# Attention and token/channel mixer on one core: a hand-planned instruction order with other durations, and the odd batches' tail mask in pieces

## The chip, the cores and the metric

One core of a Trainium2 chip runs the whole program, in one launch. The metric is the device time of that launch in microseconds (us), as the median of several runs. Five engines of the core matter: TensorE (PE in the profile, its weight loads PEld), VectorE (DVE), ScalarE (ACT), GpSimd (POOL) and SyncE (SP). In this kernel GpSimd and SyncE issue DMAs and do little else. Each engine works through its own queue in order; between engines there are semaphores.

## The reference

Eight batches, eight heads, 576 positions, 64 channels a head. Attention looks back over a window of 128 positions with a bias that falls linearly with distance (its slope differs by head); a mixer over tokens and then over channels follows.

```python
scores = scale * np.matmul(q, k.transpose(0, 1, 3, 2))
bias = slopes[:, None, None] * (-np.abs(rel).astype(np.float32))[None, :, :]
mask = (rel >= 0) & (rel < window)
scores = np.where(mask, scores + bias[None], -1000000000.0)
attn = softmax(scores); x = attn @ v            # heads side by side: 512 channels
h = np.maximum(xt @ w_tok1, 0.0) @ w_tok2       # xt: x with tokens last
u = x + h.transpose(0, 2, 1)
out = u + np.maximum(u @ w_ch1, 0.0) @ w_ch2
```

(The line with softmax stands for several of the reference.) w_tok1 is 576 x 256, w_tok2 256 x 576, w_ch1 512 x 1536, w_ch2 1536 x 512.

## The kernel before

**Tiling.** A batch has 576 = 4 x 128 + 64 positions. Two batches make a pair: four blocks of 128 rows for each, and a ninth, TAIL, that holds both remainders of 64 rows, the even batch's in rows 0 to 63 and the odd batch's in rows 64 to 127. For every block of a pair the queries and keys are loaded (GpSimd's queue, L551, cast to bf16 on the way), turned (for the first pair by TensorE against an identity, L704, and copied out of PSUM, L710; for later pairs by a transposing DMA on SyncE's queue, L693), multiplied into scores for the block and the one ahead of it (L741), put through the exponential on ScalarE (L756), multiplied on VectorE by a tile of decays that is both bias and mask (L766), multiplied by the values (L799) and divided by the row sum (reciprocal L812, product L815; ScalarE can do the product too, L821). Then the token mixer: matmuls L844 and L854, a clamp at zero L862/L863, matmuls L887 and L883, sum with x L905, and a transposition (L922 and L928, or a DMA). The odd batch's 64 tail rows lie in another half than some of the weights, so the tile xt gets a copy of them in the other half (L839). The channel mixer is the main work: matmuls L1341 with clamps L1347/L1348 in the first half, tail pieces L1384, matmuls L1519 and L1429 in the second, with sums on VectorE (L1366, L1490, and the weight sums L642 and L660) that save a product of each 2 x 2 group.

**Batch 0** has a way of its own (the function opening, from L936): its q and k for two of four head pairs come in f32 over SyncE's and ScalarE's queues into the raw tiles, and VectorE or ScalarE casts them (L584); the same for its 64 tail rows (L590).

**Masks.** ScalarE makes the decay tiles `masks[:, e, i]` (L525) for the two halves e of the heads. For the odd batches, whose tail rows sit in the upper half, VectorE builds `maskt` from them: two half-width copies (L670), one full copy (L671), one memset (L672), for each e. The first pair's odd batch and all later pairs' tails read it.

**What sets the order.** No engine's order is written by hand. `plan.op(engine, cost, emit, rank, ...)` notes each instruction group with its expected duration in ns, the buffers it makes, uses and reads, and a rank; `Plan.run` then replays the machine on the host with these costs, a model of DMA queues, PSUM banks and rings of buffers, and sends out on each engine the group that can start first, ranks breaking ties (ranks under FIRST are waited for a little). The kernel is emitted in the order that this replay gives. In that replay

- a load costs its packets times PACKET = 0.813 ns on one of two modelled queues, whose clock begins at START; its result counts as there 2790 ns after;
- `after=` forbids a start before that time, RAW_AT gives such times for the raw tiles' casts;
- `other=(engine, cost, emit)` lets a second engine do it when it would end sooner;
- VectorE is free again 80 ns before an instruction's cost is over, so neighbours overlap;
- where TensorE would stand still over 250 ns before 60 us, matmuls on a zero tile are put in (`spin`, L1577).

Batch b's main work goes side by side with batch b + 1's attention and token mixer (`side`), whose ranks are spread over part of the main work's.

Of the kernel before, what the change touches and what calls it, by code (L numbers as in the profile page):

```python
# [71 lines left out]
class Plan:  # L72
# [9 lines left out]
    def op(self, eng, cost, emit, rank, makes=(), adds=(), rewrites=(), part=None, uses=(), reads=(), needs=(),  # L82
           after=0.0, order=None, bus=0.0, other=None, mode=0, behind=()):
# [6 lines left out]
        o.order, o.bus, o.other, o.mode = order, bus, other, mode  # L90
# [42 lines left out]
    def run(self):  # L133
# [28 lines left out]
        mode, turned = 0, -1e9  # L162
# [54 lines left out]
        while todo:  # L217
            best = None
            for e, c in cand.items():
                pick, early = None, None  # L220
                for o in c:
                    if e == "POOL" and o is not pool[sent]:
                        continue
                    t = max(ready[o], free[e])
                    if o.other:
                        mine, its = (o.cost, o.other[1]) if e == o.eng else (o.other[1], o.cost)
                        that = o.other[0] if e == o.eng else o.eng
                        if max(ready[o], free[that]) + its < t + mine - (0 if e == o.eng else 1):
                            continue
# [105 lines left out]
RAW_AT = [4.4e3, 5.0e3, 6.0e3, 6.6e3, 9.0e3, 8.5e3]  # L335
# [17 lines left out]
RELU = 350  # L353
# [10 lines left out]
START = 5000.0  # L364
# [5 lines left out]
DECAYS = -3e5  # L370
MORE = 1
# [18 lines left out]
def kernel(  # L390
# [197 lines left out]
    for i in range(2):  # L588
        def cast(eng, i=i, buf=last["qk"]):
            eng(out=buf()[0:R, i, :, :], in_=ends_[i * R : (i + 1) * R, :].rearrange("p (h d) -> p h d", h=H))  # L590

        plan.op("DVE", 455, lambda cast=cast: cast(dve_.tensor_copy), -1e6 + TAIL_AT, makes=last["qk"], after=RAW_AT[4 + i],
                other=("ACT", 600, lambda cast=cast: cast(act_.copy)))
# [9 lines left out]
    for item in LOADS.split():  # L603
# [7 lines left out]
        elif what == "W":  # L611
            if n == 1:
                lw1 += weights([(W1[:, 0:NC, :], w1, 512, 1640)] +
                               [(W1p[0:R, 0, :], moe_w_tok1[NC * P : S, :], 64, 250)])
            else:
                lw2 += weights([(W2[:, :, :], w2[:, :, 0 : NC * P], 256, 2300)])
        elif what == "P":
            lw1p += weights([(W1p[R:P, 1, :], moe_w_tok1[NC * P : S, :], 64, 250)])
# [48 lines left out]
    for e in range(2):  # L667
        def go(e=e):
            for i in range(2):
                dve_.tensor_copy(out=maskt[:, e, :, 0, i * R : (i + 1) * R], in_=masks[:, e, :, 0, 0:R])  # L670
            dve_.tensor_copy(out=maskt[:, e, :, 1, :], in_=masks[:, e, :, 1, :])  # L671
            dve_.memset(maskt[0:R, e, :, 1, R:P], 0.0)  # L672
        mt.append(plan.op("DVE", 1300, go, 0, after=30e3, needs=mk_ops[e]))

# [99 lines left out]
    def values(pr, blk, half, pb, rank):  # L774
# [12 lines left out]
        for es in ([[0, 1]] if both else [[0], [1]]):  # L787
# [36 lines left out]
            plan.op("DVE", 180 + 4 * (n - 1), recip, rk, makes=rt, uses=[ot])  # L824
            plan.op("DVE", 154 + 270 * n, norm, rk, part=(xb, (blk, half)), uses=[ot, rt],
                    other=("ACT", 115 + 830 * n, norms))

    def token_mix(b, rank):
# [9 lines left out]
        if xt:  # L838
            plan.op("DVE", 395, lambda: dve_.tensor_copy(out=xt()[far, :], in_=xb()[own, TAIL, :]), rank(0),  # L839
                    makes=xt, reads=[(xb, (TAIL, tk))])  # L840
# [95 lines left out]
    def opening(rank):  # L936
# [131 lines left out]
        def ends():  # L1068
# [26 lines left out]
            def value():  # L1095
                for e in range(2):
# [8 lines left out]
                    makes=rt, uses=[ots])  # L1105
# [3 lines left out]
                part=(xb, ("t", 0)))  # L1109
# [501 lines left out]
```

## Time and profile before

| what | us |
|---|---|
| median of three runs | 279.07 (278.93 to 279.22) |
| profiled execution | 279.5 |
| its span | 277.6 |
| TensorE busy | 266.5 (96%) |
| VectorE busy | 209.7 (76%) |
| ScalarE busy | 138.4 (50%) |
| GpSimd busy | 114.7 (41%) |

The time is one of the whole launch; the span goes from the first to the last instruction that the profile shows. A row of the timeline has start, length, engine, line, operation, tiles, shapes, count, and in brackets how long the engine stood idle ahead of it and what ended that. TensorE's matmuls overlap, so the length of a row goes past the start of the next. A row of a window has the window, its length, the busy time of each engine with its count of instructions, the granted TensorE clock, the mean busy share of the DMA engines and GB/s.

### The profile page before, as it was taken

The page shows a single profiled execution, that of the slowest core. Times are in us where ns is not written, and L with a number is a line of the kernel's source. Part 1 is how long each engine was busy: PE and PEld are TensorE (multiplying, and loading weights), DVE is VectorE, ACT ScalarE, POOL GpSimd, SP SyncE. Part 2 cuts the span into 40 slices and gives each one's busy share as a digit, 9 for nine tenths or more (in the row PEclk, how much of TensorE's full clock was granted, in tenths as well). Part 3 has the DMA queues.
Part 4 walks back from the last instruction along what each step waited for, and adds up shares of the span by engine and source line. Part 5 has one row for each costly group of instructions (what it writes and reads, how often), then busy time and mean ns, then how long its engine had stood idle before and what let it go on. Part 6 is the DMA issues. An engine that isn't in the chain of part 4 may idle for free.

```text
span 277.6 us, 7099 instructions
## 1 busy us (share of the span) xinstructions
PE 266.5 (96%) x2848; PEld 182.0 (66%) x2881; DVE 209.7 (76%) x489; ACT 138.4 (50%) x219; POOL 114.7 (41%) x146
## 2 busy tenths in 40 slices
PE   5989999999999999999999999999999999999994
PEld 4676566575686655585667655586667756489983
DVE  8686789996898469674978469674979469697972
ACT  6874795136971287207951087207951087205500
POOL 8988695830297008700684008800570310022000
PEclk9999999999999999999999999999999999999998
DMA  8999999999999999999899979999899820043014
GB/s 201 178 175 179 165 153 178 148 151 198 131 134 130 171 203 85 143 153 178 147 137 157 243 133 77 149 152 188 137 132 118 211 78 2 22 110 117 2 50 140
DMA packets 160337, 38.58 MB, mean 139 GB/s; under 512 B 146544, under 2 KB 159472, under 8 KB 160304
## 3 DMA queue, kind: packets, MB, share of 16 engines
q0 software_dynamic: 109968, 19.64, 90.0%
q1 hardware_dynamic: 49264, 17.83, 35.6%
q10 hardware_dynamic: 1072, 0.66, 0.8%
q8 instruction: 22, 0.36, 0.5%
q14 instruction: 11, 0.09, 0.1%
HBM read 35.85 MB, written 9.44 MB: 163 GB/s over the span
## 4 chain that ended last, share of the span: by engine, by line
PE 86%; DVE 8%; ACT 4%; issue 1%; ACTq 0%
PE ps L1519 25%; PE ps L1341 24%; PE ps L741 5%; PE ps L799 5%; PE ps L1384 4%; PE ps L844 4%; PE ps L887 4%; PE ps L1429 4%; PE ps L1265 3%; DVE WT L642 1%; ACT r L1347 1%; ACT pe L756 1%; DVE ub L905 1%; PE ps L982 1%; DVE pe L766 1%
## 5 line engine op out<-in xcount | busy, mean ns | idle before, releaser
L1347 ACT ACTIVATE r<-ps 128x512 bf16<-128x512 f32 x73 | 43.3, 602 | 76.3 <-PE ps L1341 70.4
L1341 PE MATMUL ps<-uT,WC 128*128 128x512 bf16 x304 | 77.2, 380 | 1.0
L551 POOL DMA_DIRECT2D v<-in_v_dram x36 | 30.4, 845 | 88.0 <-PE ps L799 85.6
L756 ACT ACTIVATE pe<-ps 128x1024 bf16<-128x1024 f32 (+1 forms) x64 | 55.2, 915 | 3.7 <-PE ps L741 3.0
L1341 PEld LDWEIGHTS <-WC 128*128 128x128 bf16 x324 | 28.7, 98 | 29.2 <-issue 0.9
L1519 PEld LDWEIGHTS <-r 128*128 128x128 bf16 x384 | 37.0, 98 | 9.2 <-issue 2.4
L766 DVE TENSOR_TENSOR pe<-pe,mask 128x1024 bf16<-128x1024 bf16 (+1 forms) x56 | 34.1, 618 | 9.9 <-ACT pe L756 9.4
L551 POOL DMA_DIRECT2D qk<-in_q_dram x35 | 30.2, 866 | 5.2 <-DMA qkT<-qk 3.1
L551 POOL DMA_DIRECT2D qk<-in_k_dram x35 | 30.3, 870 | 2.9 <-DMA qk<-in_k_dram 1.4
L1519 PEld LDWEIGHTS <-s 128*128 128x128 bf16 x288 | 28.1, 98 | 4.5 <-issue 0.2
L1490 DVE TENSOR_TENSOR raw<-ps,ub 128x512 f32<-128x512 f32 x27 | 18.3, 684 | 10.4 <-PE ps L1519 10.3
L815 DVE TENSOR_TENSOR xb<-ps,rt 128x256 bf16<-128x256 f32 (+1 forms) x62 | 25.2, 418 | 0.9 <-DVE rt L812 0.2
L1519 PE MATMUL ps<-WC,r 128*128 128x256 bf16 x192 | 25.4, 273 | 0.0
L1519 PE MATMUL ps<-WT,s 128*128 128x256 bf16 x192 | 24.1, 273 | 0.0
L1519 PE MATMUL ps<-WT,r 128*128 128x256 bf16 x192 | 23.7, 273 | 0.0
L799 PEld LDWEIGHTS <-pe 128*128 128x128 bf16 (+1 forms) x480 | 18.4, 99 | 7.5 <-DVE pe L766 2.1
L799 PE MATMUL ps<-v,pe 128*128 128x65 bf16 (+1 forms) x480 | 22.2, 195 | 0.0
L905 DVE TENSOR_TENSOR ub<-ps,xb 128x512 bf16<-128x512 f32 x32 | 19.7, 681 | 2.0 <-PE ps L887 2.0
L741 PEld LDWEIGHTS <-qkT 64*128 64x128 bf16 x480 | 12.8, 94 | 9.5 <-issue 6.6
L1502 POOL DMA_DIRECT2D out_dram<-raw x6 | 4.3, 717 | 34.1 <-DVE raw L1490 34.1
L1490 DVE TENSOR_TENSOR raw<-ps,raw 128x512 f32<-128x512 f32 x19 | 12.9, 688 | 7.1 <-PE ps L1519 7.0
L741 PE MATMUL ps<-qkT 64*128 64x128 bf16 (+1 forms) x256 | 16.8, 218 | 0.8
(137 smaller groups left out, 380.8 us busy)
## 6 DMA issues: line engine op xcount, KB each, us to landing
out_dram<-raw SPq DMA_DIRECT2D x21, 256.0 KB, 2.8
qk<-in_q_dram POOLq DMA_DIRECT2D x30, 128.0 KB, 5.7
qk<-in_k_dram POOLq DMA_DIRECT2D x30, 128.0 KB, 6.0
v<-in_v_dram POOLq DMA_DIRECT2D x28, 128.0 KB, 5.9
WC<-in_moe_w_ch_dram POOLq DMA_DIRECT2D x8, 384.0 KB, 7.3
out_dram<-raw POOLq DMA_DIRECT2D x6, 256.0 KB, 2.8
v<-in_v_dram POOLq DMA_DIRECT2D x16, 64.0 KB, 4.2
out_dram<-ob SPq DMA_DIRECT2D x3, 256.0 KB, 2.7
```

The lines of the kernel that those rows point to most:

```text
L551: nc.gpsimd.dma_start(out=to()[p0 : p0 + n, :, :], in_=rows(src, b, s0, n))
L741: pe_.matmul(wide(e)[:, i, kind, a:z], lhsT=ts[kb]()[e * D : (e + 1) * D, NHP + i, :], rhs=ts[blk]()[e * D : (e + 1) * D, i, a:z], start=T ...
L756: act_.activation(out=pb()[:, e, :, lo:, c0:c1_], in_=wide(e)[:, :, lo:, c0:c1_], func=ACT.Exp, scale=scale)
L766: dve_.tensor_tensor(out=o, in0=o, in1=heads(mk, es), op=ALU.mult)
L799: pe_.matmul(view()[a:z, at, i, :], lhsT=pb()[:, e, i, kind, a:z], rhs=vb()[:, h, 0 : D + 1], start=m == 0, stop=m == len(mms) - 1, skip_g ...
L815: dve_.tensor_tensor(out=x4(), in0=view()[r0:r1_, :, :, 0:D], in1=rt()[r0:r1_, 0:n, :, :].broadcast_to([r1_ - r0, n, 4, D]), op=ALU.mult)
L844: pe_.matmul(t1[j]()[:, :], lhsT=W1[:, c, j * P : (j + 1) * P], rhs=xb()[:, blk, :], start=c == 0, stop=False)
L905: plan.op("DVE", 690, lambda blk=blk, ht=ht, hs=hs: dve_.tensor_tensor(out=ub()[:, blk, :], in0=ht()[:, hs], in1=xb()[:, blk, :], op=ALU.a ...
L1341: pe_.matmul(ct()[:, :], lhsT=WC1[:, cb, t * P : (t + 1) * P], rhs=uT()[:, cb, :], start=cb == 0, stop=cb == NCB - 1)
L1347: plan.op("ACT", 600, lambda t=t, ct=ct: act_.activation(out=r2()[:, t, :], in_=ct()[:, :], func=ACT.Relu), rk, part=(r2, t), uses=[ct], o ...
L1490: dve_.tensor_tensor(out=v, in0=bk().rearrange("p (c n) -> p c n", c=2), in1=src, op=ALU.add)
L1519: pe_.matmul(bk()[:, c * HN : (c + 1) * HN], lhsT=l(t, c), rhs=w(t), start=first, stop=g == 1 and t == HK - 1, skip_group_check=True)
```

## The change

The list of loads, the tiles and the arithmetic stay. The diff (context left out) changes four things.

1. A planner item can be marked `narrow`. VectorE's next item then starts at the earliest 31 ns after the end of the one before, if either is narrow; otherwise the overlap stays. Marked are the casts of batch 0's tail rows, the divisions of tails that cover one half (the opening's and those of the first pair), and the copy to xt.

```diff
+        mode, last = 0, (False, 0.0)
...
+                    if e == "DVE" and (o.narrow or last[0]):
+                        t = max(t, last[1] + 31.0)
...
                 o.t0, free[e], o.done = t, t + max(o.cost - 80, 50), t + o.cost
+                last = (o.narrow, o.done)
```

2. Costs and times of the replay. W1 and W1p are the first token weight, W2 the second, A0 to A3 the quarters of the first channel weight. RELU is the cost of the clamp of a sum in SBUF (L1291).

```diff
-RAW_AT = [4.4e3, 5.0e3, 6.0e3, 6.6e3, 9.0e3, 8.5e3]
+RAW_AT = [4.2e3, 4.5e3, 5.7e3, 6.1e3, 7.5e3, 7.8e3]
-RELU = 350
+RELU = 295
-START = 5000.0
+START = 4300.0
...
-                lw1 += weights([(W1[:, 0:NC, :], w1, 512, 1640)] +
-                               [(W1p[0:R, 0, :], moe_w_tok1[NC * P : S, :], 64, 250)])
+                lw1 += weights([(W1[:, 0:NC, :], w1, 512, 1560)] +
+                               [(W1p[0:R, 0, :], moe_w_tok1[NC * P : S, :], 64, 270)])
...
-                lw2 += weights([(W2[:, :, :], w2[:, :, 0 : NC * P], 256, 2300)])
+                lw2 += weights([(W2[:, :, :], w2[:, :, 0 : NC * P], 256, 1560)])
...
-            lc1 += weights([(WC1[:, :, hs], c1[:, :, hs], 512, 2500 + 1400 * (n == 0))]) * (NHT // 4)
+            lc1 += weights([(WC1[:, :, hs], c1[:, :, hs], 512, 2460)]) * (NHT // 4)
```

3. The copy to xt costs 290 in place of 395 and may go to ScalarE at 600.

```diff
-            plan.op("DVE", 395, lambda: dve_.tensor_copy(out=xt()[far, :], in_=xb()[own, TAIL, :]), rank(0),
-                    makes=xt, reads=[(xb, (TAIL, tk))])
+            plan.op("DVE", 290, lambda: dve_.tensor_copy(out=xt()[far, :], in_=xb()[own, TAIL, :]), rank(0),
+                    makes=xt, reads=[(xb, (TAIL, tk))], narrow=True,
+                    other=("ACT", 600, lambda: act_.copy(out=xt()[far, :], in_=xb()[own, TAIL, :])))
```

4. The odd batches' tail mask: one item of 1300 for each e, not before 30 us, becomes four items with a rank of their own and no such time.

```diff
+MASKT = -2e5
...
-        mt.append(plan.op("DVE", 1300, go, 0, after=30e3, needs=mk_ops[e]))
-
+        got = []
+        for i in range(2):
+            got.append(plan.op("DVE", 200, lambda e=e, i=i: dve_.tensor_copy(
+                out=maskt[:, e, :, 0, i * R : (i + 1) * R], in_=masks[:, e, :, 0, 0:R]), MASKT, needs=mk_ops[e]))
+        full = plan.op("DVE", 290, lambda e=e: dve_.tensor_copy(out=maskt[:, e, :, 1, :], in_=masks[:, e, :, 1, :]), MASKT,
+                       needs=mk_ops[e])
+        got.append(plan.op("DVE", 290, lambda e=e: dve_.memset(maskt[0:R, e, :, 1, R:P], 0.0), MASKT, needs=[full]))
+        mt += got
```

More of the change, by code (lines that the diff above doesn't have):

```diff
@@ L82, in op @@
     def op(self, eng, cost, emit, rank, makes=(), adds=(), rewrites=(), part=None, uses=(), reads=(), needs=(),
-           after=0.0, order=None, bus=0.0, other=None, mode=0, behind=()):
+           after=0.0, order=None, bus=0.0, other=None, mode=0, behind=(), narrow=False):
         def many(x):
@@ L89, in op @@
         o.t0 = o.done = None
-        o.order, o.bus, o.other, o.mode = order, bus, other, mode
+        o.order, o.bus, o.other, o.mode, o.narrow = order, bus, other, mode, narrow
         o.n = len(self.ops)
```

18 lines of the change are left out of this document (6 added, 12 removed).

## The prediction, made before the changed kernel had run

> **What bounds the kernel now.** I read the page first, then busy time by stage, then the waits of TensorE, then the timelines of the stretches where it loses time.
>
> ```profile
> span 277.6 us, 7099 instructions
> PE 266.5 (96%) x2848; PEld 182.0 (66%) x2881; DVE 209.7 (76%) x489; ACT 138.4 (50%) x219; POOL 114.7 (41%) x146
> PE 86%; DVE 8%; ACT 4%; issue 1%; ACTq 0%
> ```
>
> The reader sees a TensorE kernel: 96% busy, and 86% of the chain that ended last. The profiled execution took 279.5 us, so 1.9 us lie around its span of 277.6; the median of the runs is 279.07, 0.43 below it. Sums below are made against 279.5 and span 277.6, and 0.43 is taken off at the end. The next view has busy time by stage: start and end, length, then PE, PEld, DVE, ACT, POOL, granted clock, DMA share.
>
> ```profile
> 0.00:13.00 13.00, 9.49 (x156) 7.49 (x157) 9.71 (x39) 9.46 (x18) 12.06 (x21) 1.00 1.28 193
> 13.00:27.00 14.00, 13.20 (x214) 9.82 (x211) 10.32 (x26) 8.94 (x17) 12.09 (x15) 1.00 1.79 174
> ...
> 27.00:40.00 13.00, 12.66 (x126) 7.09 (x128) 10.18 (x29) 11.22 (x18) 10.14 (x15) 1.00 1.82 157
> 40.00:46.00 6.00, 5.87 (x103) 4.14 (x101) 5.67 (x17) 5.39 (x10) 4.12 (x5) 1.00 1.33 191
> 46.00:57.00 11.00, 10.51 (x91) 7.00 (x91) 10.68 (x22) 1.85 (x4) 7.10 (x9) 1.00 2.43 148
> ...
> 60.00:91.00 31.00, 30.64 (x354) 20.84 (x358) 26.24 (x64) 18.63 (x31) 14.32 (x17) 1.00 1.71 149
> ...
> 249.00:277.60 28.60, 24.63 (x250) 22.09 (x247) 19.14 (x37) 8.96 (x16) 2.15 (x3) 0.97 0.24 78
> ```
>
> From 60 to 91 us TensorE is idle 0.36 us of 31, and the waits view has no wait of TensorE at all between 60 and 250 us. The last stage's 4 idle us are the drain behind the last matmul. So the amount of matmul sets the time after 60 us, and a new order there is worth little: I bound it at 0.3 us either way. What an order can give lies before: 0.8 us idle from 13 to 27, 0.34 + 0.13 + 0.49 from 27 to 57, and what is busy without use, which the timeline shows (start, length, engine, line):
>
> ```profile
> 30.43 0.61 PE L704 MATMUL ps<-ident,qk 128*128 128x128 bf16 x8
> 34.99 0.61 PE L704 MATMUL ps<-ident,qk 128*128 128x128 bf16 x8
> 37.62 0.61 PE L704 MATMUL ps<-ident,qk 128*128 128x128 bf16 x8
> 41.38 1.20 PE L1577 MATMUL ps<-zero 128*128 128x512 bf16 x10
> 42.70 0.66 PE L1577 MATMUL ps<-zero 128*128 128x512 bf16 x6
> 50.19 0.37 PE L854 MATMUL ps<-xt,W1p 64*128 64x512 bf16 x1 [0.38 <-DVE xt L839]
> ```
>
> L1577 is filler on a zero tile, emitted where the planner expects TensorE to have nothing. The next useful matmuls start at 42.44 and 43.43, so the two fillers stand for 1.06 + 0.73 = 1.8 us. The last row is the one wait on another engine after 30 us, 0.38. With the 0.96 idle (0.38 of it this wait) some **2.8 us** can be won from 27 to 57 at most. In 46 to 57 VectorE is busy 10.68 of 11 us and ScalarE 1.85: one engine is full beside an empty one, and the chain of waits runs over VectorE there.
>
> **The change part by part.**
>
> *Load times.* The diff starts the modelled queue of loads at 4300 instead of 5000, and makes the second token weight 740 units and the first channel weight 1440 units cheaper, at 0.813 ns a unit. All together, with small parts of 65 and 33 ns, what follows them is expected 0.70 + 0.07 + 0.60 + 1.17 + 0.1 = 2.6 us sooner. Against that stand the loads as they landed (the issue's row, then size and us from issue to landing):
>
> ```profile
> 20.34 0.91 POOL L551 DMA_DIRECT2D qk<-in_k_dram  x1
> 23.99 0.89 POOL L551 DMA_DIRECT2D qk<-in_k_dram  x1 [0.23 <-issue]
> 27.10 0.89 POOL L551 DMA_DIRECT2D qk<-in_k_dram  x1
> ```
>
> ```profile
> qk<-in_k_dram POOLq DMA_DIRECT2D x1, 128.0 KB, 7.3
> qk<-in_k_dram POOLq DMA_DIRECT2D x1, 128.0 KB, 8.7
> qk<-in_k_dram POOLq DMA_DIRECT2D x1, 128.0 KB, 8.2
> ```
>
> The keys of blocks 5, 6 and 7 landed at 27.64, 32.69 and 35.30; their transposes (L704 above) stand at 30.43, 34.99 and 37.62, so 2.8, 2.3 and 2.3 us after. An order that believes in loads 2.6 us sooner takes them 0.2 us after landing, and 0.3 us before it twice. Each of those two costs at most 0.3 us of TensorE. What it gives: scores and exponentials of batch 1 begin up to 2.5 us sooner, ahead of the stretch from 40 us in which TensorE was fed fillers. The ends are -2.3 (1.8 of filler and 0.47 idle from 27 to 46) and +0.6 (two waits, nothing won). I take **-1.0**, about half the filler, since ScalarE, which must do those exponentials, was 11.22 of 13 us busy from 27 to 40 us.
>
> *Tail mask.* Two planner items of 1300 become eight small ones, free of the rule that held them until 30 us.
>
> ```profile
> L670 DVE COPY maskt<-mask x4: 154/212/221, 29.5 to 30.3; 128x256 bf16<-128x256 bf16 x4
> L671 DVE COPY maskt<-mask x2: 280/284/288, 29.7 to 30.4; 128x512 bf16<-128x512 bf16 x2
> L672 DVE MEMSET maskt<- x2: 165/165/165, 30.1 to 30.8; 64x128 uint32 x2
> 32.67 0.56 DVE L1366 TENSOR_TENSOR s<-r 128x768 bf16<-128x768 bf16 x1 [1.75 <-ACT r L1347]
> ```
>
> The instructions are the same eight, 4 x 212 + 2 x 284 + 2 x 165 = 1.75 us, less by overlap (29.45 to 30.92). Leaving that place frees nothing by itself: the next VectorE work at 32.67 waited 1.75 us for ScalarE. It does clear the place where block 5's copy and masks now want to go. In the opening the pieces fill holes: VectorE had one of 1.79 us before 8.41.
>
> ```profile
> 8.41 0.69 DVE L960 COPY qkT<-ps 128x512 bf16<-128x512 bf16 x1 [1.79 <-PE ps L957]
> 9.13 0.87 DVE L590 CAST qk<-raw 64x512 bf16<-64x512 f32 x2
> ```
>
> The same hole takes the two casts of L590. Their sources, issued at 1.75 and 1.80 us, landed in 5.6 and 5.9:
>
> ```profile
> raw<-in_q_dram SPq DMA_DIRECT2D x1, 128.0 KB, 5.6
> raw<-in_k_dram ACTq DMA_DIRECT2D x1, 128.0 KB, 5.9
> ```
>
> That is 7.35 and 7.70, while the casts ran at 9.13. Moving them up and the pieces in leaves VectorE's load in the opening about as it was, so I cost both at **0**, hidden by that hole and by later ones of 0.2 to 0.4 us. Without that cover the pieces cost 1.5 us between 13 and 27 us, where TensorE waits on VectorE already; a gain of 0.3 is the other end, when the casts' old place goes to the copies.
>
> *What else the pieces could meet.* One copy of L839 shows it:
>
> ```profile
> L839 DVE COPY xt<-xb x7: 286/289/587, 49.5 to 207.3; 64x512 bf16<-64x512 bf16 x7
> ```
>
> ```profile
> 31.25 0.71 POOL L572 DMA_DIRECT2D W2t<-in_moe_w_tok_dram  x1 [1.68 <-DMA WC<-in_moe_w_ch_dram]
> ...
> 49.14 0.88 POOL L551 DMA_DIRECT2D qk<-in_q_dram  x1
> ```
>
> The median of seven is 289 ns; the longest, 587, is the first, at 49.55, and GpSimd was issuing a load from 49.14 to 50.02. GpSimd was busy 12.06 of the first 13 us, and idle 1.68 us up to 31.25, beside the pieces' old place. So a copy moved forward may cost 0.3 us more, and six of them 1.8. [...]
>
> *VectorE beside half tiles.* The planner let VectorE instructions overlap by 80 ns; it now keeps 31 ns between one marked narrow and its neighbours.
>
> ```profile
> 48.50 0.43 DVE L815 TENSOR_TENSOR xb<-ps,rt 64x256 bf16<-64x256 f32 x1
> 48.96 0.56 DVE L642 TENSOR_TENSOR WT<-WC,WT 128x768 bf16<-128x768 bf16 x1
> 49.55 0.59 DVE L839 COPY xt<-xb 64x512 bf16<-64x512 bf16 x1
> ```
>
> That is the truth of batch 1's tail: 48.50 + 0.43 = 48.93, the next at 48.96, and from 49.52 the next at 49.55. The hardware's time is not changed by believing it, but the order is. The half-tile copy to xt (L839, 49.55) may now go to ScalarE, which was empty there:
>
> ```profile
> 49.84 0.60 ACT L862 ACTIVATE r<-ps 128x512 bf16<-128x512 f32 x1 [3.86 <-PE ps L854]
> ```
>
> ScalarE sat idle 3.86 us before 49.84. Its input was ready at 48.93, so a ScalarE copy of 0.60 ends near 49.6 instead of 50.14, ahead of the clamp at 49.84 that would stand behind it in ScalarE's queue, and the 0.38 us wait of TensorE goes. VectorE also loses 0.62 us from a full stretch, so the sums of L905 behind it come sooner; TensorE had other matmuls then, and I count nothing for it. Value **-0.4**; ends 0 (VectorE is chosen again) and -0.5 (all that was idle from 46 to 57).
>
> *The rest.* A cheaper final clamp (350 to 295) and casts allowed 0.2 to 1.5 us sooner change places, not work: 0, from -0.3 to +0.5. The list of loads is untouched, so nothing passes anything else in GpSimd's queue.
>
> *What is late next.* The sum is -1.4. A floor stands behind it: batch 2's tail scores need a transposing DMA on SP's queue (issue, its time to landing, and the matmuls that use it).
>
> ```profile
> 73.33 2.44 SPq L693 DMA_TRANSPOSE qkT<-qk  x1
> ```
>
> ```profile
> qkT<-qk SPq DMA_TRANSPOSE x1, 4.5
> ```
>
> ```profile
> 79.10 0.23 PE L741 MATMUL ps<-qkT 64*128 64x128 bf16 x2
> ```
>
> It landed at 77.83, and the matmuls ran at 79.10: **1.27 us** of room. DMA share is 1.82, 1.33 and 2.43 from 27 to 57 us, so I do not expect that landing to move. With G won before 60 us, TensorE waits G - 1.27 there, and nothing gives that back. Net: -1.3, so 279.5 - 1.3 = 278.2 for a profiled run, and **277.8** for the median. With one term at its bad end and the others as taken, the sum is +0.2, 279.3 (loads); +0.1, 279.2 (pieces uncovered); +0.4, 279.5 (copies); -1.0, 278.1 (xt); or -0.9, 278.2 (the rest).
>
> **The rivals.**
>
> 1. *The floor gives way* (15%). Buffers of blocks 4 to 7 come free sooner, loads with them, and 1.8 of filler, 0.4 of xt and 0.3 of the opening are all kept: 279.07 - 2.5 = **276.6**. For it: the loads go through a ring of five buffers. Against it: a DMA share over 1, which is backlog and not late issue.
> 2. *The change does not do what it says* (17%). Loads are believed sooner, but ScalarE sets batch 1's pace (5.39 of 6 us from 40 to 46), so the fillers stay: only part of xt's 0.38 is won, and small losses of moved order eat half: **278.9**.
> 3. *Blocked copies* (5%). All six copies cost 0.3 more and lie on the path: 279.07 - 1.4 + 1.8 = **279.5**. The trace has one such copy in seven. [...]
> 4. *TensorE's queue is stopped by batch 2's tail scores* (18%), the slower side. If the order also pulls them forward by p of TensorE's work, because their loads too are believed sooner, TensorE stands at its head waiting for 77.83, with everything behind it. The net is then p - 1.27: slower than before from p = 1.27, and at most 2.6 - 1.27 = +1.3. Taken in the middle of what is slower, p = 2.2: **280.0**. For it: a model that is 2.6 us sooner passes the 2.3 us lag of blocks 6 and 7, so it is too hopeful late. Against it: the tail's place follows from a rank that spreads side work over main work, and 1.27 us of room was there.
>
> **How the numbers follow.** The forecast, 277.2 to 278.5, has 45%. A measurement of this kernel tells about 0.2% from no change, 0.56 us: faster is below 278.51, slower above 279.63. Faster: 45 + 15 + 4 of rival 2 = 64%. Same: 13 of rival 2, 3 of rival 3 = 16%. Slower: 18 + 2 = 20%. The likeliest is 277.8. The range goes from rival 1's time, 276.6, to rival 4's, 280.0; half of each lies outside, with a little for sums of bad ends: 2 in 10.
>
> **What would show it.** Load step right: L704 of blocks 5 to 7 within 0.5 us of 27.6, 32.7 and 35.3, and filler of L1577 after 40 us under 1 us; wrong: two fillers of 1.8 us again. Mask step: L670 to L672 between 6 and 25 us, each piece near 0.21, 0.28 and 0.17 us; near 0.5 speaks for rival 3. xt: its first copy on ScalarE, and no wait of L854. Floor: the matmuls of batch 2's tail within 0.2 us of the landing of their transpose; a wait over 1.3 us there is rival 4. The stretch 96 to 249 us should keep its length within 0.3 us; if it changes by more, the argument that TensorE alone sets it is wrong, and with it the prediction.

## The result, and the profile after

| | before | after |
|---|---|---|
| median, runs side by side on one chip | 279.15 (278.86 to 279.7, 14 runs) | 277.5 (276.7 to 278.89, 14 runs) |
| profiled execution | 279.5 | 277.12 |
| its span | 277.6 | 275.1 |

The ratio is 0.9942 with an interval of [0.9926, 0.9958]: 1.65 us less, and clear of the 0.2% that can be told from no change. The runs of the changed kernel spread over 2.2 us, those of before over 0.8. Six further runs of the changed kernel in another series gave 277.9 (276.81 to 278.79) against 279.44, ratio 0.9938 [0.9913, 0.9963]. One of the twelve runs of the kernel without load times (see the table below), 285.05 us at a mean granted clock of 0.988, was a slow one and is left out of its row.

All lines of the code behind the diff's first hunk stand 5 or 6 lower than in before (L704 is L709, L1577 is L1583, L741 is L746). The page of the changed kernel: span, TensorE, and the shares of the chain that ended last.

```profile
span 275.1 us, 7113 instructions
...
PE 265.2 (96%) x2855; PEld 182.2 (66%) x2888; DVE 211.6 (77%) x492; ACT 136.9 (50%) x222; POOL 114.5 (42%) x146
...
PE 91%; DVE 5%; issue 1%; ACT 1%; ACTq 0%; DVEq 0%
```

TensorE still bounds it. Its windows (the window, its length, busy time of each engine, granted clock, DMA share, GB/s):

```profile
0.00:13.00 13.00, 9.87 (x154) 7.51 (x155) 10.22 (x43) 9.34 (x17) 12.06 (x21) 1.00 1.27 193
13.00:27.00 14.00, 13.18 (x229) 10.65 (x232) 12.10 (x33) 8.71 (x16) 11.79 (x15) 1.00 1.80 175
27.00:40.00 13.00, 12.84 (x155) 7.81 (x157) 10.72 (x27) 10.34 (x15) 10.88 (x15) 1.00 1.84 164
40.00:46.00 6.00, 5.95 (x75) 3.49 (x74) 5.90 (x16) 3.84 (x13) 3.79 (x6) 1.00 1.43 189
46.00:57.00 11.00, 10.95 (x91) 7.58 (x92) 10.55 (x21) 3.94 (x7) 8.21 (x10) 1.00 2.17 156
60.00:91.00 31.00, 30.79 (x366) 22.09 (x369) 26.95 (x64) 18.64 (x32) 13.88 (x17) 1.00 1.74 161
249.00:275.10 26.10, 22.11 (x226) 19.84 (x224) 17.65 (x34) 7.79 (x14) 0.64 (x1) 0.97 0.21 68
```

From 27 to 57 us TensorE now stands still for 0.16 + 0.05 + 0.05 = 0.26 us, before 0.96. Busy is not the same as useful, though: fillers count as busy. The rows of TensorE's timeline that answer to those shown of before are three key transposes (blocks 5, 6 and 7), the only filler behind 27 us, and the tail's two matmuls (one reads xt) that had waited:

```profile
28.54 0.61 PE L709 MATMUL ps<-ident,qk 128*128 128x128 bf16 x8
...
32.73 0.61 PE L709 MATMUL ps<-ident,qk 128*128 128x128 bf16 x8
...
35.18 0.62 PE L709 MATMUL ps<-ident,qk 128*128 128x128 bf16 x8
...
43.64 0.51 PE L1583 MATMUL ps<-zero 128*128 128x128 bf16 x6
...
46.03 0.39 PE L860 MATMUL ps<-xb,W1p 64*128 64x512 bf16 x1
46.03 0.39 PE L860 MATMUL ps<-xt,W1p 64*128 64x512 bf16 x1
```

The transposes come 1.9 to 2.4 us sooner. Of the 1.86 us of filler behind 40 us there is 0.51 left, and the wait of 0.38 us for xt is gone. But the windows of the filler line alone show that the opening got some (the window, its length, TensorE busy with L1583); before had none in this window:

```profile
18.00:27.00 9.00, 1.68 (x16) 1.00 (x17) 1.00 1.91 177
```

To see what a stretch won or lost whatever its mix, I count **loss**: the length of a stretch less the matmuls of the computation that begin in it, each at the step at which its shape follows itself in the trace at full clock (216 ns for 512 columns, 109 for 256, 56 for 128, 31 for 65 and so on; 251.3 us in every kernel). What is left is idle time, filler, half clock and slow pace (128 columns step at 105 ns ahead of the first full grant, which the trace has at 6.49 us in before). Some traces (before and after among them) lack 32 records of matmuls of 512 columns that the others have; these are counted in. A matmul at the edge of a stretch falls to one side or the other, so differences of 0.2 between two rows tell nothing. Time is the median of the runs, the four stretches are of the profiled execution, us:

| kernel | median (range, runs) | ratio to before, interval | 0-27 | 27-57 | 57-96 | 96-end |
|---|---|---|---|---|---|---|
| before | 279.15 to 279.44 in four series | | 11.27 | 4.88 | 0.82 | 5.08 |
| after | 277.5 (276.7 to 278.89, 14) | 0.9942 [0.9926, 0.9958] | 11.92 | 1.73 | 1.12 | 4.75 |
| after, again | 277.9 (276.81 to 278.79, 6) | 0.9938 [0.9913, 0.9963] | 12.56 | 1.75 | 0.89 | 4.92 |
| load times alone | 279.81 (279.31 to 281.45, 10) | 1.003 [1.0011, 1.0049] | 12.22 | 3.81 | 0.93 | 4.95 |
| mask pieces alone | 280.65 (279.39 to 281.59, 10) | 1.0043 [1.0026, 1.006] | 12.38 | 5.26 | 1.05 | 4.95 |
| narrow and xt alone | 285.39 (284.8 to 285.77, 4) | 1.0217 [1.0201, 1.0232] | 11.05 | 4.24 | 7.76 | 4.88 |
| after without load times | 280.72 (280.11 to 284.08, 11) | 1.0067 [1.0042, 1.0091] | 11.14 | 4.57 | 2.12 | 5.04 |
| after without mask pieces | 281.09 (280.83 to 281.35, 4) | 1.0064 [1.0049, 1.0079] | 11.92 | 3.38 | 2.56 | 5.76 |
| after without narrow | 279.54 (278.22 to 281.94, 12) | 1.0009 [0.9983, 1.0034] | 12.26 | 2.27 | 1.76 | 5.99 |
| after, pieces at 20 us | 277.13 (276.82 to 278.47, 6) | 0.9921 [0.9899, 0.9943] | 11.92 | 1.63 | 1.01 | 4.83 |
| after's order, mask put back | 277.24 (276.56 to 278.19, 6) | 0.993 [0.9915, 0.9944] | 11.85 | 1.47 | 1.01 | 4.87 |
| after's order, xt put back | 278.24 (277.2 to 278.83, 8) | 0.9958 [0.9941, 0.9976] | 11.88 | 1.76 | 1.12 | 4.77 |
| before's order, mask early | 279.3 (278.85 to 279.54, 11) | 1.0001 [0.9993, 1.001] | 11.27 | 4.88 | 0.82 | 5.07 |
| pieces at 20 us, W first | 277.23 (276.9 to 280.88, 12) | 0.994 [0.9916, 0.9963] | 11.92 | 1.73 | 1.12 | 4.74 |

So the change wins 3.15 us between 27 and 57 us, gives back 0.65 in the opening and 0.3 in 57 to 96, and wins 0.33 at the end: 2.53 in all; the two spans differ by 2.5. (The last two are near what an edge can do.) By 65 us all of it is there: the first score group (L746) behind 60 us starts at 65.55, before at 67.19, 1.64 sooner, and with one chunk of the channel mixer more behind it (four matmuls of 216 ns, 0.86), 2.5 in all.

### The profile page after: what moved, and what is told of

Read it like the earlier page. It is cut to its first block, busy times and chain, and to the rows that moved or that the text cites. A ratio compares the mean times of both kernels' runs of the same rounds, so it can differ in the third digit from the quotient of the medians.

```text
span 275.1 us, 7113 instructions
## 1 busy us (share of the span) xinstructions
PE 265.2 (96%) x2855; PEld 182.2 (66%) x2888; DVE 211.6 (77%) x492; ACT 136.9 (50%) x222; POOL 114.5 (42%) x146
## 4 chain that ended last, share of the span: by engine, by line
PE 91%; DVE 5%; issue 1%; ACT 1%; ACTq 0%; DVEq 0%
PE ps L1525 27%; PE ps L1347 25%; PE ps L804 6%; PE ps L746 6%; PE ps L850 4%; PE ps L893 4%; PE ps L1390 4%; PE ps L1435 4%; PE ps L1271 3%; PE ps L709 1%; PE ps L1333 1%; PE ps L860 1%; PE ps L889 1%; PE ps L928 1%; PE ps L1154 1%
## 5 line engine op out<-in xcount | busy, mean ns | idle before, releaser
L1353 ACT ACTIVATE r<-ps 128x512 bf16<-128x512 f32 x71 | 42.0, 601 | 75.4 <-PE ps L1347 69.3
L820 DVE TENSOR_TENSOR xb<-ps,rt 128x256 bf16<-128x256 f32 (+1 forms) x60 | 24.2, 418 | 0.6
L746 PEld LDWEIGHTS <-qkT 64*128 64x128 bf16 x480 | 12.8, 94 | 8.5 <-issue 6.1
L746 PE MATMUL ps<-qkT 64*128 64x128 bf16 (+1 forms) x256 | 16.7, 218 | 0.4
```

What stands on the lines that cost most here:

```text
L746: pe_.matmul(wide(e)[:, i, kind, a:z], lhsT=ts[kb]()[e * D : (e + 1) * D, NHP + i, :], rhs=ts[blk]()[e * D : (e + 1) * D, i, a:z], start=T ...
L820: dve_.tensor_tensor(out=x4(), in0=view()[r0:r1_, :, :, 0:D], in1=rt()[r0:r1_, 0:n, :, :].broadcast_to([r1_ - r0, n, 4, D]), op=ALU.mult)
L1353: plan.op("ACT", 600, lambda t=t, ct=ct: act_.activation(out=r2()[:, t, :], in_=ct()[:, :], func=ACT.Relu), rk, part=(r2, t), uses=[ct], o ...
```

## The experiments

**First series: each part alone, and the whole without its mask.** Three theories: A, the load times carry the gain; B, VectorE's corrected replay (narrow, xt) carries it; C, the mask's old place would hold most of it back.

*Load times alone*: the kernel before with these figures.

```diff
-RAW_AT = [4.4e3, 5.0e3, 6.0e3, 6.6e3, 9.0e3, 8.5e3]
+RAW_AT = [4.2e3, 4.5e3, 5.7e3, 6.1e3, 7.5e3, 7.8e3]
-START = 5000.0
+START = 4300.0
-                lw1 += weights([(W1[:, 0:NC, :], w1, 512, 1640)] +
+                lw1 += weights([(W1[:, 0:NC, :], w1, 512, 1560)] +
...
```

The other weights' costs are those of the change too; RELU keeps the figure of before in all three single parts.

> Before plus the load times alone (START, the costs of the token and channel weights, RAW_AT); no narrow rule, xt as before, tail mask as before at 30 us. Theory A, the load times carry the gain: batch 1's transposes move up to within 0.5 us of the landing of their keys and the fillers after 40 us go, 1.0 to 1.5 us below the kernel before, with the wait of the xt matmul (0.4 us) still there. Theory B, the replay of VectorE carries it: within 0.4 us of the kernel before. Theory C, the mask's old place is what holds the gain back: the transposes move, but the time stays within 0.4 us of before.

Measured 279.81, no gain. In 27 to 57 us the loss fell by 1.07. But the opening's rose by 0.95, part of it between 18 and 27 us, where the windows of the filler line alone now show filler, as in after:

```profile
18.00:27.00 9.00, 1.20 (x13) 0.67 (x11) 1.00 1.92 177
```

So the load times win what was expected of them where it was expected, and the order that they bring loses it ahead of that. A falls as a theory of the whole.

*Mask pieces alone*: before, with the eight pieces in place of the two items.

```diff
-        mt.append(plan.op("DVE", 1300, go, 0, after=30e3, needs=mk_ops[e]))
+            got.append(plan.op("DVE", 200, lambda e=e, i=i: dve_.tensor_copy(
+                out=maskt[:, e, :, 0, i * R : (i + 1) * R], in_=masks[:, e, :, 0, 0:R]), MASKT, needs=mk_ops[e]))
...
```

> Before plus the tail mask in eight early pieces alone. Theories A and B: within 0.3 us of the kernel before, since the next work on VectorE at 32.67 us waited for ScalarE anyway. Theory C: 0.7 us or more below it. The pieces should run before 25 us, and where GpSimd is issuing loads take up to 0.5 us longer than the 0.21 and 0.28 us of before.

Measured 280.65. The profiled run (281.1) shows a fall of the granted clock that I had not looked for. Windows of it, chosen at the edges of its clock record:

```profile
5.54:8.96 3.42, 2.12 (x48) 1.50 (x47) 3.04 (x12) 3.16 (x7) 3.42 (x5) 1.00 1.65 195
8.96:12.37 3.41, 3.24 (x39) 2.50 (x39) 1.82 (x7) 2.76 (x4) 3.41 (x6) 0.50 1.71 183
```

TensorE was busy 2.12 of 3.42 us, and for the next 3.41 us its granted clock is 0.50. Four of the ten runs show a mean clock of 0.992 or 0.993 over the span, and these four are 280.74 to 281.59; the three of 279.39 to 279.94 show 0.998 and over. The other three lie at 280.48 to 280.67 with 0.997 to 0.999, so the clock is a part of the loss and not all of it.

*Narrow and xt alone*: before, with point 1 and point 3 of the change.

> Before plus the narrow rule and the copy to xt at 290 with ScalarE allowed; nothing else. Theory A: 0.2 to 0.5 us below the kernel before (the one wait of 0.38 us goes). Theory B: 1.2 us or more below it.

Measured 285.39, 6.2 us slower: the wait of rival 4, longer than rival 4 had it. TensorE's timeline and windows, and the time to landing of the transposing DMA (issued at 73.48) that TensorE waited for:

```profile
79.95 0.29 PE L744 MATMUL ps<-qkT 64*128 64x128 bf16 x2 [3.79 <-DMA qkT<-qk]
```

```profile
75.80:79.21 3.41, 0.36 (x2) 0.00 (x0) 1.40 (x3) 1.08 (x3) 1.80 (x3) 1.00 2.05 156
79.21:82.62 3.41, 2.67 (x42) 2.04 (x43) 0.79 (x4) 1.60 (x2) 0.35 (x1) 0.50 1.91 165
82.62:86.04 3.42, 3.42 (x14) 1.83 (x13) 2.49 (x6) 1.26 (x5) 2.29 (x3) 0.50 0.95 109
```

```profile
qkT<-qk SPq DMA_TRANSPOSE x1, 6.4
```

TensorE came to the tail's scores at 76.16, 2.9 us sooner than before ran them (79.10), as rival 4 describes. With before's landing at 77.83 that would be a wait of 1.7 us. The DMA was issued when before issued it (73.33), but took 6.4 us instead of 4.5; so 2.0 of the 3.79 us are a late landing, which rival 4 does not have. TensorE's queue stands there for 3.79 us, and then the granted clock is 0.50 in two windows, 6.83 us together: by estimate (half of them) up to 3.4 us more, 7.2 in all. The table has 6.9 more than before in 57 to 96. In this execution GpSimd was also held for 1.71 us ahead of its load at 9.90; before has no such wait there, and no run shows whether the two belong together. How long a wait has to be for the clock to fall is not shown.

*After without mask pieces*: the changed kernel with the two items of 1300 from 30 us put back, the order written anew by the planner.

> The changed kernel with the tail mask put back to two items of 1300 at 30 us. Theory A: within 0.4 us of the changed kernel, about 277.5 to 277.9. Theory C: back near 279.1, since the mask stands where block 5's copies and masks now want to go.

Measured 281.09. All three theories are at odds with this table: no part alone is faster than before, and the whole without one of its parts is slower than before. In this variant filler stands at another place:

```profile
48.58 1.79 PE L1581 MATMUL ps<-zero 128*128 128x512 bf16 x12
```

Two explanations are left. **D**: the loads' place and the mask's VectorE work are two limits of the same stretch, and both have to go. **E**: the list planner's order answers to every figure, and each variant falls into a wait of its own; what a variant loses says nothing of the work that the part takes away.

**Second series: the other two parts left out, the pieces later, and the changed kernel again.**

*After without load times* (START 5000, the old weights' costs and RAW_AT).

> The kernel after with the load times, the weights' costs and the opening's arrival times put back to those of before (START 5000, 1640/250/2300/2500+1400, RAW_AT 4.4 to 9.0); mask pieces, narrow rule and the second engine for xt stay. Theory D (two limits of 27 to 57 us have to go together: the late loads' place in the order, and the 2.6 us of mask work on VectorE; whichever stays is the next limit): the loads' place stays the limit, L709 of batch 1 comes near 30.4, 35.0, 37.6 as in before, the loss of TensorE in 27-57 stays at 4 us or more, 280.0 to 281.0. Theory E (the planner's list order reacts to any figure, and each variant falls into a wait of its own, with nothing common): 279 to 285, and the loss sits at one wait that has nothing to do with the loads, as in the variant with the narrow rule alone. Theory F (mask out and narrow rule carry it and the load figures do little): 277.5 to 278.2.

Measured 280.72. TensorE's timeline:

```profile
30.17 0.61 PE L710 MATMUL ps<-ident,qk 128*128 128x128 bf16 x8
...
41.16 1.20 PE L1584 MATMUL ps<-zero 128*128 128x512 bf16 x10
42.68 0.66 PE L1584 MATMUL ps<-zero 128*128 128x512 bf16 x6
50.98 0.94 PE L1584 MATMUL ps<-zero 128*128 128x512 bf16 x8
77.98 0.23 PE L747 MATMUL ps<-qkT 64*128 64x128 bf16 x2 [1.29 <-DMA qkT<-qk]
```

The key transpose of block 5 is back at 30.17 (before 30.43), and the two fillers are back, with a third. The loss in 27 to 57 us is 2.84 more than in after. So the load times are needed for the gain: F, by which they do little, falls. The 2.84 is not their price, though: the third filler is new, and block 5's key itself landed later in this order (29.21, in after 27.75). The wait of 1.29 us at 77.98 is rival 4 again, smaller.

*After without narrow* (the rule of 31 ns and its marks taken out, xt's second engine kept).

> The kernel after without the rule that keeps narrow VectorE operations apart (mode flag narrow gone); load times, mask pieces and xt's second engine stay. Theory D: the two limits are gone as in after, and the rule only shifts the order by 31 ns steps: 277.3 to 278.3, loss of TensorE in 27-57 between 1.5 and 2.5 us, transposing DMA of batch 2's rest issued near 70.6. Theory E (any figure taken back gives another order and a wait of its own): 279 or more, with a wait of TensorE of over 1 us somewhere behind 57 us, or the transposing DMA of the rest late.

Measured 279.54, where D had 277.3 to 278.3. TensorE's waits from 8 to 250 us (line, releaser, us in all, times, longest):

```profile
PE ps L1104 <- DVE pe L1092: 1.5, 1, 1.5
PE ps L1345 <- DMA uT<-ub: 1.0, 1, 1.0
PE ps L1523 <- ACT pe L759: 0.5, 1, 0.5
```

They lie at 17.28, 120.86 and 80.55 us. The second and third stand far behind the narrow work of the opening: another order, with other waits. That is E's sign, if only just (it asked for a wait of over 1 us behind 57 us); D does not foresee it. The first and longest lies among the opening's narrow work, so it may be the rule's own worth; this run can't tell.

*Pieces at 20 us*: after, each piece with one more argument.

```diff
-                out=maskt[:, e, :, 0, i * R : (i + 1) * R], in_=masks[:, e, :, 0, 0:R]), MASKT, needs=mk_ops[e]))
+                out=maskt[:, e, :, 0, i * R : (i + 1) * R], in_=masks[:, e, :, 0, 0:R]), MASKT, needs=mk_ops[e], after=20e3))
...
```

> The kernel after, with the eight mask pieces held back until 20 us in the planner's order (they go into VectorE's holes of 20 to 27 us) instead of running at 5.7 and 13.6 to 16.5 us. Theory H (the pieces ahead of the second pair of casts cost 0.5 us of TensorE at 7.1 us, and the thin opening is what spreads the runs of after over 2.2 us): that wait is gone, loss of TensorE in 0-27 falls from 11.9 to about 11.3, time 276.9 to 277.1 and spread under 1.2 us. Theory I (the opening's loss comes from the clock's grant, 7.36 us against 6.49 in before, and the order of the casts, not from the pieces): loss in 0-27 within 0.3 of 11.9, 277.3 to 277.7, spread near 2 us. If the pieces cost VectorE at 20-27 what they saved: 277.8 or more, with waits of TensorE on L715 or L1177 there.

This bears on the pieces' price in the opening. In after they were dear, and they pushed the casts (sources, two rows of VectorE, one of TensorE):

```profile
L674 DVE COPY maskt<-mask x4: 339/403/759, 5.7 to 15.0; 128x256 bf16<-128x256 bf16 x4
...
L676 DVE COPY maskt<-mask x2: 274/515/756, 6.1 to 15.2; 128x512 bf16<-128x512 bf16 x2
```

```profile
5.69 0.47 DVE L674 COPY maskt<-mask 128x256 bf16<-128x256 bf16 x2
...
6.54 0.82 DVE L588 CAST qk<-raw 128x512 bf16<-128x512 f32 x2
```

```profile
7.08 0.53 PE L963 MATMUL ps<-ident,qk 128*64 128x128 bf16 x8 [0.52 <-DVE qk L588]
```

With the pieces at 20 us the matmuls of L963 come 0.26 us sooner, with a shorter wait for another engine, yet the loss in 0 to 27 us is the same 11.92, as theory I has it:

```profile
6.82 0.64 PE L963 MATMUL ps<-ident,qk 128*64 128x128 bf16 x8 [0.25 <-ACT qkT L966]
7.39 0.93 PE L1004 MATMUL ps<-qkT 64*128 64x128 bf16 x14
```

The next group, L1004, took 0.93 us here and 0.56 in after (where it starts at 7.54): in the trace's record the first full clock is granted at 8.24 in this execution, at 7.36 in that of after. By 9.0 us the two are level again. The filler of 0 to 27 us is the same, 4.3 us in both. 277.13 and a spread of 1.65 us lie between H and I; against the changed kernel's 277.9 in the same series the intervals overlap, so it is not shown to be better.

*After, again.*

> The kernel after unchanged, on the same chip as the three others, for a second profiled execution and more times. Its times so far lie between 276.7 and 278.89. If the spread comes from the clock's window in the opening, the first full grant of this profile differs from 7.36 us and the loss in 0-27 differs from 11.92 by about as much as its time differs from 277.12; the rest of the span keeps its loss (1.74, 1.12, 4.63) within 0.2 us. If it comes from DMA landings, a wait or filler behind 27 us differs instead.

The second profiled execution took 277.79, 0.67 more than the first. Its loss differs in the opening alone (12.56 against 11.92, 0.64). The cause is neither the clock (its first full grant stands at 7.36 us in the first and 7.14 in the second in the trace's record, and it does not fall back in either) nor anything behind 27 us, but a landing: GpSimd's issue of the first token weight, and TensorE's wait for it.

```profile
8.93 0.76 POOL L576 DMA_DIRECT2D W<-in_moe_w_tok_dram  x1 [0.51 <-DMA v<-in_v_dram]
```

```profile
W<-in_moe_w_tok_dram POOLq DMA_DIRECT2D x1, 256.0 KB, 5.9
```

```profile
14.91 0.62 PE L1126 MATMUL ps<-xb,W 128*128 128x128 bf16 x8 [0.67 <-DMA W<-in_moe_w_tok_dram]
```

In the first execution W was issued at 8.19 and landed 5.0 later, at 13.2, ahead of its matmul at 14.17: 1.0 us of room. Here it was issued 0.74 later, after a wait for an older load to land, and took 5.9: 14.83. The trace's record of semaphores says which: GpSimd's loads share eight, and the tenth, W, has the one of the second, v. That v landed at 7.84 in the first execution and at 8.64 here, 0.29 us ahead of W's issue (9.62 with narrow and xt alone, 0.28 ahead, where the hold was 1.71 us). Before used W at 14.98 at the earliest, so it had 1.8 us of room. The new order stands closer to a transfer that varies.

**Third series: one instruction group moved, the rest of the order held.** If E is right, leaving a part out of the planner's input can't price it. So the plan was made as ever, and then only the place of the group in the program was changed; TensorE's stream of instructions is the same word for word.

*After's order, mask put back.* D and E part here.

```diff
     plan.run()
+    for e, at in enumerate((30000.0, 31220.0)):
+        for i in range(4):
+            plan.ops[149 + 4 * e + i].t0 = at + i
     plan.emit(spin)
```

> The order of the kernel after, kept instruction for instruction on every engine, with one thing changed: the eight mask pieces leave their early places on VectorE and stand together ahead of the first L1354 behind 30 us, where the kernel before had them. Theory D (the mask's 1.5 us of VectorE work in 27-57 is itself what the earlier loads are short of): loss of TensorE in 27-57 rises from 1.7 to about 3.2 us, 278.7 to 279.2. Theory E (the early mask earns nothing by its work, since VectorE sat idle for 1.49 us just there, before 32.07 us; what the variant with the mask put back by the planner lost, it lost by the other order that the planner then wrote): loss in 27-57 within 0.3 of 1.7, 277.2 to 277.8.

Measured 277.24, loss in 27 to 57 us 1.47: E. VectorE in after had this row:

```profile
32.07 0.69 DVE L1354 TENSOR_SCALAR r<-ps 128x512 bf16<-128x512 f32 x1 [1.49 <-PE ps L1347]
```

and with the mask back:

```profile
30.14 0.35 DVE L674 COPY maskt<-mask 128x256 bf16<-128x256 bf16 x2
...
31.43 0.17 DVE L678 MEMSET maskt<- 64x128 uint32 x1
31.71 0.69 DVE L1354 TENSOR_SCALAR r<-ps 128x512 bf16<-128x512 f32 x1
```

The mask, 30.14 to 31.60, fills the hole in which VectorE waited for TensorE. The same move made through the planner had cost 3.6 us (281.09): none of that was the mask's work.

*Before's order, mask early* (the two blocks moved to 6.95 and 26.15 us).

```diff
     plan.run()
+    plan.ops[149].t0, plan.ops[150].t0 = 7000.0, 25900.0
     plan.emit(spin)
```

> The order of the kernel before, kept instruction for instruction, with one thing changed: the two mask blocks leave VectorE's stretch of 29.5 to 30.9 us; the first goes ahead of the first L960 (VectorE's hole of 1.79 us that ends at 8.41), the second ahead of the first L766 (hole of 0.95 us that ends at 27.14). Theory D or E alike: with the late loads VectorE waits 1.75 us for ScalarE behind the old place in any case, so nothing is won in 27-57: loss there 4.6 to 5.0, 279.0 to 279.6. If the block in the opening is blocked beside GpSimd as the pieces of the kernel after were and runs past 8.4 us, the opening loses up to 0.5 more: up to 279.9. The mask's early place worth something by itself: 278.5 or less.

Measured 279.3 against 279.21, ratio 1.0001 [0.9993, 1.001]. The hole behind the old place grew from 1.75 to 3.13 us, and nothing came of it:

```profile
32.71 0.56 DVE L1366 TENSOR_TENSOR s<-r 128x768 bf16<-128x768 bf16 x1 [3.13 <-ACT r L1347]
```

*After's order, xt put back* (batch 1's copy issued on VectorE at the same place of the program).

> The order of the kernel after, kept instruction for instruction, with batch 1's copy of the tail (xt, L844/L846) issued on VectorE at the same place of the program instead of ScalarE. The prediction's term for it was 0.4 us: if it holds, TensorE waits again for VectorE ahead of L860 or L893 near 46 us, 0.3 to 0.5 us, 277.8 to 278.0 in median. If ScalarE's copy is hidden anyway, no wait appears and the time is that of the kernel after within 0.2 us (277.3 to 277.8).

No wait came back ahead of L860 or L893. One appears later, of 0.29 us:

```profile
52.64 0.83 PE L1525 MATMUL ps<-WT,s 128*128 128x256 bf16 x6 [0.29 <-DVE s L1372]
```

The profiled run took 277.24 with the loss of after (1.76 against 1.73 in 27 to 57 us); the median of eight is 278.24, with four runs at 277.2 to 277.8 and four at 278.68 to 278.83. Against 277.24 with the mask back in the same series the intervals touch. So xt on ScalarE is worth between nothing and 1.0 us here; it stays open.

*Pieces at 20 us, W first*: GpSimd issues W one place earlier.

```diff
     plan.run()
+    plan.ops[29].t0, plan.ops[30].t0 = plan.ops[30].t0, plan.ops[29].t0
     plan.emit(spin)
```

> The kernel after with the mask pieces at 20 us (277.13 in the last series, 276.82 to 278.47), kept instruction for instruction, with one thing changed: on GpSimd's queue the first load of the token weights W goes ahead of the value load that stood before it, so that it is issued 0.7 us earlier. Theory J (the runs of the kernel after spread because W's landing, 0.7 us late in the second profile of it, then holds TensorE at 14.2 us, with about 1 us of room in a good run): spread falls under 1 us, median 276.7 to 277.0. If the spread comes from elsewhere: median 277.0 to 277.4 and a spread of 1.5 us as before. If the value load, 0.8 us later, is what is late next: a wait of TensorE on L1047 or L1106 and 277.5 or more.

Measured 277.23 (eleven runs from 276.9 to 278.13 and one of 280.88): J's narrower spread is not there. The run does not test J, either: in its profiled execution W was issued at 7.47 and landed 5.7 us later, at 13.1, as in the execution with the pieces at 20 us (issued at 8.21, landed at 13.1), so the move made no room. W's landing explains the one slower execution that was profiled; that it makes the spread is not shown. Over three series no variant is shown to beat the changed kernel; the three with the mask pieces elsewhere (at 20 us, put back, and W first) equal it within their intervals and beat before.

## Why the prediction was right, and where not

It gave 277.8 and 1.3 us faster; measured are 277.5 and 1.65. The direction, the place (27 to 57 us) and the mechanism held. That the number came out so close is in part luck: the profiled executions show 3.15 us won between 27 and 57 us, where 1.4 was forecast, 0.65 lost in the opening, where 0 was, and no floor. Two steps failed, the opening and the floor.

- **Load times, -1.0: right mechanism, mis-sized.** Blocks 6 and 7 are transposed at 32.73 and 35.18, within 0.15 us of the forecast 32.7 and 35.3; block 5 at 28.54, 0.9 late of 27.6. They stand 0.8, 0.5 and 0.4 us behind the landings of their keys (27.75, 32.24 and 34.81), so TensorE waited for none of them, where two waits were feared. Filler behind 40 us fell to 0.51, under the 1 us named. Alone the load times win 1.07 in their stretch. Without them the whole loses 2.84 there, beyond the end of -2.3, because two fillers and a third come back; by E that is what another order costs, and their own share lies between and stays open.
- **The opening, 0: failed as a step.** "Moving them up and the pieces in leaves VectorE's load in the opening about as it was" priced VectorE's load, which is not what TensorE lost there. The opening lost 0.65 in after and 0.95 with the load times alone, without any pieces, and no less with the pieces at 20 us. Its new filler stands between 18 and 27 us (1.68, before 0.00): the third group of W's matmuls, at 18.18 in before (L1120), comes at 20.43 (L1126), and filler takes its place. Which of the load figures does that was not tried.
- **Tail mask, 0: right, and shown from both sides**: early in before's order +0.1, late in after's order 277.24. The reason given, that the next VectorE work waits anyway, is what the 3.13 and the 1.49 us show.
- **Blocked copies: they did run longer, and the price was near nil.** The forecast had each piece near 0.21, 0.28 and 0.17 us and named 0.5 as the sign of rival 3; the longest took 0.759, 0.756 and 0.165. GpSimd was busy 12.06 of the first 13 us. The half-width copies took 403 ns in the median, against 212 at the old place. The other orders go the same way: at 20.8 to 22.8 us, beside GpSimd's issues, the median is 320 (longest 659); with the mask put back, at 30.1 to 30.9 us, where GpSimd issued nothing between 29.94 and 31.09, it is 212 again. The memset did not lengthen (165 ns in both). That the copies run longer beside GpSimd's issues is what these runs show; why is not shown. Rival 3's 279.5 did not follow: the pieces pushed a cast that TensorE waited for, but by 0.26 us, and that was gone by 9 us.
- **xt, -0.4: the wait went as described** (ScalarE's copy, no wait of L860). With the copy put back the wait does not come back there: in the new order it was hidden, and the term is not shown as a gain of its own.
- **The narrow rule: no price of its own.** "The hardware's time is not changed by believing it, but the order is" was right, but the sum has no term for that order beside xt's: the whole without the rule is 279.54, 2.0 slower, with waits at 17, 80 and 120 us. **The rest, 0** (the cheaper clamp and the casts' times), no run tried alone.
- **The floor: failed.** "I do not expect that landing to move." SyncE's transposing DMA of batch 2's rest (SPq is SyncE's queue), its time to landing, the matmuls, and the load of the last key that it turns, as issued by GpSimd, with its time to landing:

```profile
70.64 1.24 SPq L698 DMA_TRANSPOSE qkT<-qk  x1
```

```profile
qkT<-qk SPq DMA_TRANSPOSE x1, 4.3
```

```profile
77.25 0.23 PE L746 MATMUL ps<-qkT 64*128 64x128 bf16 x2
```

```profile
59.58 0.68 POOL L555 DMA_DIRECT2D qk<-in_k_dram  x1 [1.67 <-DMA qk<-in_k_dram]
```

```profile
qk<-in_k_dram POOLq DMA_DIRECT2D x1, 64.0 KB, 10.9
```

  The same load in before:

```profile
61.02 0.68 POOL L551 DMA_DIRECT2D qk<-in_k_dram  x1 [1.38 <-DMA qk<-in_k_dram]
```

```profile
qk<-in_k_dram POOLq DMA_DIRECT2D x1, 64.0 KB, 12.2
```

  The transposing DMA was issued at 70.64, 0.13 us behind that key's landing at 70.51 (before 73.33 and 73.18). It landed at 74.9 (before 77.83) and was used at 77.25: 2.3 us of room, more than before. The key's load was issued 1.44 us sooner, because GpSimd waits there for earlier transposes (which free buffers) and earlier loads (which free semaphores: the load eight ahead, with the same one, landed at 59.30, in before at 60.73), and these waits ended sooner: the one for a transpose at 55.55, in before at 57.58. It also took some 1.2 us less to land; why is not shown. So the DMA share over 1 (1.82, 1.33 and 2.43 from 27 to 57 us) that I read as backlog fixed no time: the issue moved with the work, and the landing moved by more. Nothing was capped at 1.3, and rival 1's mechanism is what happened: 2.4 us between the two profiled executions.
- **From 2.4 to 1.65.** The profiled execution of after was one of its better ones, 0.4 under its median, and that of before 0.35 over its own. The forecast took the second into account and could not know the first.
- **Rival 4 was the right thing to fear.** It did not happen in after (no wait of TensorE behind 30 us), but its neighbours have it: 1.29 us without the load times, and 3.79 with narrow and xt alone, 2.0 of it from a late landing. **Rival 2** did not happen: the fillers went.
- **96 to 249 us kept its length**: from batch 3's first score group to the end it is 277.6 - 97.34 = 180.3 before and 275.1 - 94.81 = 180.3 after.

What stays open: why the runs of after and its relatives spread by 1.2 to 2.2 us (one run at 280.88 apart), beyond the one case of W, where those of before spread by 0.7 to 1.9 in the four series; which load figure brings the filler of 18 to 27 us; and the shares of the load times, the narrow rule and xt in the gain.

## What to carry to other kernels

Where a planner writes the order, leaving one figure out measures another order, and not the part: the mask's place cost 3.6 us that way and nothing when it alone was moved. To price a part, hold the order and move that one group; to judge a set of figures, run the set. And ask of a transfer that looks like a floor what its issue waits for: if it waits for buffers that the faster work releases, it moves along.

## What the hardware showed that was not expected

The granted clock fell to 0.50 after a stretch of 3.42 us in which TensorE was busy for 2.12 us (mask pieces alone), while other executions kept theirs. The first row is of before; the other two are of after without narrow, one window and the next:

```profile
6.49:9.90 3.41, 2.48 (x52) 1.68 (x48) 1.56 (x4) 3.36 (x7) 3.40 (x6) 1.00 1.78 177
```

```profile
13.71:17.12 3.41, 2.05 (x54) 1.75 (x50) 3.33 (x8) 2.94 (x4) 2.92 (x4) 1.00 1.43 152
17.12:20.53 3.41, 3.22 (x62) 2.78 (x63) 3.05 (x11) 1.65 (x4) 2.48 (x3) 1.00 1.84 174
```

So the fall needed no wait as long as the 3.79 us with narrow and xt alone: the waits in the window ahead of it were 0.24, 0.68 and most of one of 0.55 us. But the busy time of a window, as the profile models it, does not decide alone: 2.12 us lost the clock and 2.05 kept it. What does decide is not shown. The cost, by estimate from the granted 0.50, is half of 3.41 us, 1.7 us at most, from an order that only looks a little thinner (2.12 us busy, in before 2.48). The half clock stood for 3.41 us here (8.96 to 12.37) and for 6.83 with narrow and xt alone (79.21 to 86.04). The edges of the clock record lay at another place in each execution (6.49 in before, 5.54 with mask pieces alone); whether that is why four of the ten runs with the mask pieces alone show a mean clock of 0.992 or 0.993, and six do not, is not shown.
